# Moving low halves to GpSimd: pooled keys and values, block 0's max-layer values, block 1's tokens

## The chip, the cores and the metric

One core of one Trainium2 chip runs the program. The metric is the time of one execution in microseconds (us) on the device; the span of the profile, from the first to the last instruction, lies inside it. The engines are PE (TensorE, matmuls), PEld (TensorE's weight loads, which overlap PE), DVE (VectorE), ACT (ScalarE), POOL (GpSimd) and SP (SyncE, which issues most transfers).

## What is computed

Three layers follow one another: attention over keys and values that are pooled by 8, a layer that takes the maximum of three products, and a layer with a squared ReLU. The inputs q, k and v are normal draws (q and k of size 0.8, v of 0.1); all is float32.

```python
# q, k, v: (8, 8, 576, 64); pool = 8
k_p = k.reshape(B, H, Sp, pool, D).mean(axis=3)
v_p = v.reshape(B, H, Sp, pool, D).mean(axis=3)
scores = scale * np.matmul(q, k_p.transpose(0, 1, 3, 2))
attn = softmax(scores)                      # over the 72 pooled keys
x = np.matmul(attn, v_p)                    # then (B * S, H * D) = (4608, 512)
h = np.maximum(np.maximum(x @ w1, x @ w2), x @ w3)      # d_ff 768
y = h @ w_out                                           # (4608, 512)
g = np.maximum(y @ w_in, 0.0)                           # d_ff 2048
out = (g * g) @ w_out2
```

## The kernel before

**Halves.** PE multiplies in a rounded float32 form, so each operand is kept as two tiles, a high half (the rounded value) and a low half (the value less its high half), and each product is three matmuls: high by high, high by low, low by high (`PARTS`, line 41). The helper `split_to` (line 120) writes the high half with a copy on ACT (line 121) and the low half with a subtraction on an engine that the caller names (line 122); `split` (line 124) does so for one tile, by default on DVE. `split_scaled` (line 194) does the same for pooled keys and values and multiplies on the way: the scale lies in ACT's copy (line 195) and in DVE's subtraction (line 196).

**First stage.** The 4608 tokens go through attention and the max layer in 12 blocks of 384 (`T1`). `attention(j)` puts the attention steps of block j into a list, each with a due time (line 272): load, prepare, scores with softmax, transposes, values. `moe1(j)` (line 453) is a generator with 22 steps for a block: 18 products (6 slices f of 128 columns by 3 weights, 12 matmuls each, line 465) whose maximum is gathered in `hm` by ACT (line 471) and DVE (line 473), the split of `hm` into `h` after the third (line 475), and 4 products with the output weights (18 matmuls each, line 484). `run` (line 494) emits the steps of all blocks in the order of due times, attention of block j + 1 among the steps of block j. Loads lead by 10 steps, preparation by 4 (line 49). What each engine then does first is set by the planner of the framework, which orders each engine's queue by its own estimate of when an instruction can start; on the chip every queue runs in that order.

**Keys and values.** For each of 32 pairs of heads (4 in each of 8 batches) `prepare_k` (line 219) sums 8 neighbouring keys on DVE into `ks` (line 221; 2 buffers) and writes high and low halves into `kbd`, 64 partitions at a time. `prepare_v` (line 226) does so with values into `vs` (line 228; 2 buffers) and `vst`, for batches 1 to 7, that is 28 pairs; batch 0's values are pooled by matmuls (`pool_v`, line 244). `kbd` and `vst` have one place for each of four pairs, so a new pair waits until the matmuls of the batch before have read it.

**Tokens.** `values` (line 376) multiplies the weights of the softmax by `vst`; from batch 1 on DVE adds two results into `xf` (line 399) and splits it into `x` on line 400. Blocks 0 and 1 (`LIGHT`, `light`) have their queries split on POOL already (line 330); block 1 holds 192 tokens of batch 1, so 4 tiles go through line 400 there.

**Weights.** Weights arrive as 64-bit numbers in 512 KB pieces, in a ring of four `raw` buffers that keys and values share for as long as the weights of the max layer arrive (`place`, line 113). `convert` (line 136) turns a piece into float32 with two ACT copies (lines 148, 149) and two DVE operations (lines 150, 153); POOL writes its low half (line 122). 24 pieces for the max layer come at the start; 32 pieces for the last layer are prepared during blocks 2 to 10, each paced by a one-element POOL copy that reads the newest `hm` (lines 132, 147).

**POOL's queue** before the change: the low halves of queries of blocks 0 and 1, those of all weights, the softmax's multiplication by 1/sum (line 355), and the pacing copies. The second stage, from about 785 us on, uses no POOL.

Of the kernel before, what the change touches and what calls it, by code (L numbers as in the profile page):

```python
# [84 lines left out]
def attention_moe_kernel(ctx: ExitStack, tc: tile.TileContext, q, k, v, vn, w1, w2, w3, wo1, wi2, wo2, out):  # L85
    nc = tc.nc
# [37 lines left out]
    def split(hl, src, engine=nc.vector):  # L124

        split_to(hl[:, 0], hl[:, 1], src, engine)
# [58 lines left out]
    kbd = kv_p.tile([P, NPAIR, 2, 2, SP], F32R, name="kbd")  # L185
# [33 lines left out]
    def prepare_k(p, kr):  # L219
        ks = sm_p.tile([P, SP], F32, tag="ks", name="ks", bufs=2)  # L220
        nc.vector.tensor_reduce(out=ks, in_=kr.rearrange("p (a b) -> p a b", b=POOL), axis=AX.X, op=ALU.add)
        for h in range(2):
            r = slice(h * D, (h + 1) * D)
            split_scaled(kbd[r, p, 0, h], kbd[r, p, 1, h], ks[r], K_SCALE)

    def prepare_v(p, vr):
        vs = sm_p.tile([SP, 2, D], F32, tag="vs", name="vs", bufs=2)
        nc.vector.tensor_reduce(out=vs, in_=vr, axis=AX.X, op=ALU.add)
        split_scaled(vst[:, p, 0:4:3], vst[:, p, 1:3], vs, V_SCALE)

    def load_natural(b):

# [74 lines left out]
    def attend(j, b, s0, n, p, t):  # L307
# [67 lines left out]
        def values():  # L375
# [16 lines left out]
            for h in range(2):  # L392
# [4 lines left out]
                r, o = slice(h * D, (h + 1) * D), slice((1 - h) * D, (2 - h) * D)  # L397
                nc.scalar.activation(xf[r], av[o], AF.Copy)
                nc.vector.tensor_tensor(out=xf[r], in0=av[r], in1=xf[r], op=ALU.add)
            split(x, xf)  # L400

        return load, prepare, softmax, transpose, values

# [49 lines left out]
    def moe1(j):  # L453
# [3 lines left out]
        for f in range(KF1):  # L457
            hm = t_p.tile([P, T1], F32, tag="hm", name="hm")
            h = h_p.tile([P, 2, T1], F32R, tag="h", name="h")
            for e in range(NE):  # L460
                ps = mm_ps.tile([P, T1], F32, tag="ps", name="ps")
                n = 0
                for kk in range(KD):
                    for a, c in PARTS:
                        nc.tensor.matmul(  # L465
                            ps, lhsT=w1_t[f, e][:, a, kk * P : (kk + 1) * P], rhs=x[kk][:, c],
                            start=(n == 0), stop=(n == 3 * KD - 1),
                        )
                        n += 1
                if e == 0:  # L470
                    nc.scalar.activation(hm, ps, AF.Copy)
                else:
                    nc.vector.tensor_tensor(out=hm, in0=ps, in1=hm, op=ALU.max)  # L473
                if e == NE - 1:
                    split(h, hm)
                yield
            hs.append(h)
            now[0] = hm
# [250 lines left out]
```

## Time and profile before

| | us |
|---|---|
| median of 3 runs (1546.5 to 1547.54) | 1547.14 |
| the profiled execution | 1546.39 |
| its span | 1544.7 |
| PE busy in the span (9290 matmuls) | 1509.4 |
| DVE busy | 948.2 |
| ACT busy | 623.5 |
| POOL busy | 199.4 |

An engine's busy time is the sum of its instructions' durations, and an instruction that waits for a port after it has begun counts as busy. Ends of matmuls are modelled. In a line of groups stand the line, engine, operation, what is written and read, the shape and the count, then the sum of busy time, the mean of one in ns, and the idle time of the engine just before them with what ended it. A timeline row begins with the start and the duration in us; in brackets stands the idle time before it and what ended it. "Issue" is time in which an engine waited for nothing that the profile shows.

### The profile page before, as it was taken

To read this page: it belongs to the slowest core of one execution; us is meant where nothing else is said; L and a number is where in the kernel's file an instruction comes from. 1 tells how busy PE (TensorE), PEld (TensorE's weight loads), DVE (VectorE), ACT (ScalarE), POOL (GpSimd) and SP (SyncE) were. 2 spreads that over 40 slices of the span, in tenths; PEclk is the share of its full clock that TensorE was granted. 3 is DMA by queue.
4 is the path that set the end of the run, shared out by engine and by line. 5 is a ranking of instruction groups with operands and counts; after the bars stand their busy time and mean duration, and the time that the engine had idled before them with its cause. 6 is when DMAs were issued, how large, how long until landed. Compare 5 with 4: busy or idle time off the path is not lost.

```text
span 1544.7 us, 25098 instructions
## 1 busy us (share of the span) xinstructions
PE 1509.4 (98%) x9290; PEld 1413.8 (92%) x9290; DVE 948.2 (61%) x1991; ACT 623.5 (40%) x1772; POOL 199.4 (13%) x303
## 2 busy tenths in 40 slices
PE   6899999999999999999999999999999999999998
PEld 4789999999999999999999898988989888999987
DVE  6895678776776767755427555455655546464544
ACT  7875566656666556654212212121212112121211
POOL 5541122222222121322000000000000000000000
PEclk7799999999999999999999999999999999999999
DMA  7552234434334332323475424333333433343331
GB/s 226 159 172 68 76 105 149 145 95 143 122 119 143 97 132 99 102 77 123 135 289 208 150 109 164 110 121 123 112 137 124 150 123 108 111 150 109 137 109 69
DMA packets 80858, 200.87 MB, mean 130 GB/s; under 512 B 9024, under 2 KB 32576, under 8 KB 80736
## 3 DMA queue, kind: packets, MB, share of 16 engines
q1 hardware_dynamic: 73824, 189.83, 36.1%
q10 hardware_dynamic: 6912, 9.44, 1.7%
q8 instruction: 74, 1.21, 0.3%
q14 instruction: 48, 0.39, 0.1%
HBM read 157.29 MB, written 41.94 MB: 129 GB/s over the span
## 4 chain that ended last, share of the span: by engine, by line
PE 85%; DVE 5%; DMA 5%; ACT 2%; issue 2%; SPq 0%; POOL 0%; DVEq 0%; ACTq 0%; POOLq 0%
PE ps L465 25%; PE acc L645 25%; PE ps L600 21%; PE ps L484 9%; PE sc L344 2%; DMA out_dram<-o 2%; PE tr L370 2%; DMA wraw<-in_w_dram 1%; PE av L396 1%; PE av L395 1%; DVE wbits L153 1%; DMA vr<-in_v_dram 1%; DMA wraw<-in_wo_dram 1%; DMA kq<-in_k_dram 1%; DVE wbits L150 0%
## 5 line engine op out<-in xcount | busy, mean ns | idle before, releaser
L465 PE MATMUL ps<-x,w 128*128 128x384 f32 x2592 | 507.6, 343 | 1.8 <-DVE x L122 1.0
L465 PEld LDWEIGHTS ps<-x,w 128*128 128x128 f32 x2592 | 451.1, 191 | 3.9 <-DVE x L122 2.0
L645 PE MATMUL acc<-wo2s,g 128*128 128x512 f32 x1728 | 412.5, 391 | 0.0
L600 PEld LDWEIGHTS ps<-y,wi2s 128*128 128x128 f32 x3024 | 370.4, 188 | 12.5 <-PE ps L600 3.4
L600 PE MATMUL ps<-y,wi2s 128*128 128x256 f32 x3024 | 376.8, 280 | 2.8 <-DVE s L629 2.2
L645 PEld LDWEIGHTS acc<-wo2s,g 128*128 128x128 f32 x1728 | 316.2, 188 | 62.6
L121 ACT ACTIVATE g<-c 128x512 fp32r<-128x512 f32 x144 | 90.8, 630 | 410.4 <-DVE c L611 403.6
L617 DVE TENSOR_TENSOR s<-ps,s 128x512 f32<-128x512 f32 x72 | 49.8, 692 | 262.2 <-PE ps L600 261.6
L484 PE MATMUL ps<-h,wo 128*128 128x384 f32 x864 | 165.2, 339 | 0.5 <-DVE hm L473 0.4
L484 PEld LDWEIGHTS ps<-h,wo 128*128 128x128 f32 x864 | 148.9, 188 | 1.3 <-DVE hm L473 0.7
L617 DVE TENSOR_TENSOR c<-ps,s 128x512 f32<-128x512 f32 x144 | 99.0, 688 | 24.9 <-PE ps L600 21.7
L355 POOL TENSOR_TENSOR ss<-ss,st 128x144 f32<-128x144 f32 (+3 forms) x144 | 74.2, 517 | 308.7 <-DVE st L354 238.6
L473 DVE TENSOR_TENSOR hm<-ps,hm 128x384 f32<-128x384 f32 x144 | 79.5, 552 | 54.2 <-PE ps L465 50.3
L349 ACT ACTIVATE ss<-sc,st 128x72 f32<-128x72 f32 (+1 forms) x320 | 98.3, 314 | 33.3 <-DVE st L346 30.8
L122 DVE TENSOR_TENSOR g<-c,g 128x512 fp32r<-128x512 f32 x144 | 98.8, 686 | 17.3 <-ACT g L121 16.4
L611 DVE SCALAR_TENSOR_TENSOR c<-c 128x512 f32<-128x512 f32 x144 | 99.0, 688 | 2.2
L373 DVE TENSOR_TENSOR pt<-tr,pt 72x256 fp32r<-72x256 f32 (+1 forms) x160 | 61.5, 387 | 52.6 <-ACT pt L372 51.2
L344 PEld LDWEIGHTS sc<-kbd,qs 128*128 128x128 f32 (+1 forms) x480 | 73.3, 191 | 12.3 <-issue 5.3
L344 PE MATMUL sc<-kbd,qs 128*128 128x144 f32 (+1 forms) x480 | 73.9, 269 | 9.2 <-ACT kbd L195 5.3
L372 ACT ACTIVATE pt<-tr 72x256 fp32r<-72x256 f32 (+1 forms) x160 | 56.4, 355 | 58.9 <-PE tr L370 57.4
L370 PE MATMUL tr<-ident,ss 128*72 128x128 f32 (+1 forms) x320 | 59.2, 271 | 13.9 <-DVE pt L373 8.8
L349 ACT ACTIVATION_READ_ACCUMULATOR ss<-sc,st 128x1 f32 (+1 forms) x320 | 63.4, 198 | 0.0
(78 smaller groups left out, 1247.0 us busy)
## 6 DMA issues: line engine op xcount, KB each, us to landing
wo2s<-wo_dram SPq DMA_DIRECT2D x144, 512.0 KB
wi2s<-wi_dram SPq DMA_DIRECT2D x24, 512.0 KB
wraw<-in_wo_dram SPq DMA_DIRECT2D x22, 512.0 KB
wraw<-in_w_dram SPq DMA_DIRECT2D x18, 512.0 KB
y_dram<-ys ACTq DMA_DIRECT2D x48, 192.0 KB
out_dram<-o SPq DMA_DIRECT2D x36, 256.0 KB
wraw<-in_wi_dram SPq DMA_DIRECT2D x16, 512.0 KB
wi_dram<-wraw SPq DMA_DIRECT2D x16, 512.0 KB
```

Source lines behind the costliest of these rows:

```text
L121: nc.scalar.activation(hi, src, AF.Copy)
L122: engine.tensor_tensor(out=lo, in0=src, in1=as_f32(hi), op=ALU.subtract)
L344: nc.tensor.matmul(src[:, i], lhsT=lhsT, rhs=kbd[:, p, l], start=(n == 0), stop=(n == 2))
L349: nc.scalar.activation(ss[:, i, h], src[:, i, h], AF.Exp, bias=st[:, 0, i, h : h + 1], accum_out=st[:, 1, i, h : h + 1],)
L370: nc.tensor.transpose(tr[:, h, :m], sms[c][:, h], ident[:m, :m])
L465: nc.tensor.matmul(ps, lhsT=w1_t[f, e][:, a, kk * P : (kk + 1) * P], rhs=x[kk][:, c], start=(n == 0), stop=(n == 3 * KD - 1),)
L473: nc.vector.tensor_tensor(out=hm, in0=ps, in1=hm, op=ALU.max)
L484: nc.tensor.matmul(ps, lhsT=wo1_t[kk][:, a, d * P : (d + 1) * P], rhs=hs[kk][:, c], start=(n == 0), stop=(n == 3 * KF1 - 1),)
L600: nc.tensor.matmul(bank[:, u * HT : (u + 1) * HT], lhsT=wi2_t[2 * gr + u][i][:, a, o + kk * P : o + (kk + 1) * P], rhs=y_t[j][m][:, c, kk] ...
L611: nc.vector.scalar_tensor_tensor(out=c, in0=c, scalar=0.0, in1=c, op0=ALU.max, op1=ALU.mult)
L617: nc.vector.tensor_tensor(out=c, in0=bank, in1=other, op=ALU.add)
L645: nc.tensor.matmul(acc_t[j][2 * half + i], lhsT=g[:, a, u * HT + i * P : u * HT + (i + 1) * P], rhs=wo2_t[j, 4 * gr + 2 * u + h][:, c], st ...
```

## The change

`prepare_k` and `prepare_v` multiply `ks` and `vs` by their scale in place on POOL, and then split them with `split_to`, whose low half is written by POOL; ACT's copies lose their scale. `split_scaled` remains for batch 0's values (`pool_v`). The low half of `x` is written by POOL in blocks 0 and 1 where a batch is 1 or later (4 tiles), and that of `h` in block 0 (6 tiles).

```diff
     def prepare_k(p, kr):
         ks = sm_p.tile([P, SP], F32, tag="ks", name="ks", bufs=2)
         nc.vector.tensor_reduce(out=ks, in_=kr.rearrange("p (a b) -> p a b", b=POOL), axis=AX.X, op=ALU.add)
+        nc.gpsimd.tensor_scalar_mul(ks, ks, K_SCALE)
         for h in range(2):
             r = slice(h * D, (h + 1) * D)
-            split_scaled(kbd[r, p, 0, h], kbd[r, p, 1, h], ks[r], K_SCALE)
+            split_to(kbd[r, p, 0, h], kbd[r, p, 1, h], ks[r], nc.gpsimd)
 
     def prepare_v(p, vr):
         vs = sm_p.tile([SP, 2, D], F32, tag="vs", name="vs", bufs=2)
         nc.vector.tensor_reduce(out=vs, in_=vr, axis=AX.X, op=ALU.add)
-        split_scaled(vst[:, p, 0:4:3], vst[:, p, 1:3], vs, V_SCALE)
+        nc.gpsimd.tensor_scalar_mul(vs, vs, V_SCALE)
+        split_to(vst[:, p, 0:4:3], vst[:, p, 1:3], vs, nc.gpsimd)
...
-            split(x, xf)
+            split(x, xf, nc.gpsimd if light else nc.vector)
...
                 if e == NE - 1:
-                    split(h, hm)
+                    split(h, hm, nc.vector if j else nc.gpsimd)
```

## Rows read from the trace of the kernel before

**Rows 1.** Windows: PE, PEld, DVE, ACT, POOL busy (count), clock, DMA share, GB/s.
```profile
0.00:118.00 118.00, 93.41 (x468) 79.49 (x469) 97.87 (x197) 90.10 (x297) 62.23 (x62) 0.84 0.58 184
118.00:735.00 617.00, 613.25 (x3787) 604.33 (x3786) 421.01 (x1120) 366.82 (x1199) 137.14 (x241) 1.00 0.34 112
```

**Rows 2.** Windows of stretches within the first 118 us, the same columns.
```profile
100.00:105.00 5.00, 2.97 (x15) 2.37 (x16) 4.94 (x7) 3.08 (x7) 3.35 (x3) 0.88 0.34 82
105.00:110.00 5.00, 5.00 (x27) 5.00 (x26) 5.00 (x13) 4.34 (x17) 0.32 (x1) 0.78 0.57 168
80.00:100.00 20.00, 18.93 (x115) 17.49 (x112) 19.40 (x40) 18.29 (x50) 11.31 (x10) 1.00 0.57 194
```

**Rows 3.** Chain of work, 0 to 118 us: start, us, what.
```profile
13.58 0.10 DVE kbd L196
13.72 0.94 DVE kbd L196
...
69.31 4.82 DMA wraw<-in_w_dram
...
98.97 2.01 DVE h L122
...
113.46 0.47 DVE h L122
```

**Rows 4.** Timeline of PE: two waits in the first block.
```profile
101.90 0.36 PE L395 MATMUL av<-pt,vst 72*128 72x192 f32 x1 [2.09 <-DVE xf L399]
...
115.11 4.11 PE L484 MATMUL ps<-h,wo 128*128 128x384 f32 x22 [0.36 <-DVE hm L473]
```

**Rows 5.** Groups of DVE, 0 to 118 us, shapes apart.
```profile
L150 DVE SCALAR_TENSOR_TENSOR wbits<-wbits,wraw 128x512 int32<-128x512 int32 x24 | 21.7, 913 | 1.2 <-ACT wraw L149 0.9 <-issue 0.2
L153 DVE SCALAR_TENSOR_TENSOR wbits<-wraw,wbits 128x512 int32<-128x512 int32 x24 | 18.7, 784 | 0.1
...
L196 DVE SCALAR_TENSOR_TENSOR kbd<-ks,kbd 64x72 fp32r<-64x72 f32 x18 | 7.0, 389 | 0.7 <-ACT kbd L195 0.4
...
L122 DVE TENSOR_TENSOR h<-hm,h 128x384 fp32r<-128x384 f32 x5 | 4.2, 844 | 0.4 <-ACT h L121 0.4
...
L196 DVE SCALAR_TENSOR_TENSOR vst<-vs,vst 72x128 fp32r<-72x128 f32 x4 | 1.6, 396 | 0.0
```

**Rows 6.** Groups of POOL, 0 to 118 us, shapes apart.
```profile
L122 POOL TENSOR_TENSOR qs<-qr,qs 128x192 fp32r<-128x192 f32 x8 | 6.9, 862 | 2.7 <-issue 1.5 <-ACT qs L121 1.1
...
L122 POOL TENSOR_TENSOR qs<-kq,qs 128x384 fp32r<-128x384 f32 x4 | 4.8, 1192 | 10.6 <-ACT qs L121 10.6
```

**Rows 7.** Groups of the whole span, shapes apart.
```profile
L122 DVE TENSOR_TENSOR g<-c,g 128x512 fp32r<-128x512 f32 x144 | 98.8, 686 | 17.3 <-ACT g L121 16.4
...
L355 POOL TENSOR_TENSOR ss<-ss,st 128x144 f32<-128x144 f32 x84 | 39.7, 475 | 200.2 <-DVE st L354 161.8 <-ACT pt L372 8.2 <-ACT ss L349 6.9
...
L132 POOL COPY wraw<-hm 1x1 f32<-1x1 f32 x32 | 7.8, 244 | 20.8 <-DVE hm L473 16.1 <-DMA wi_dram<-wraw 2.5 <-DMA wo_dram<-wraw 1.2
```

**Rows 8.** Timeline of DVE and POOL, 64 to 68 us.
```profile
64.04 3.57 DVE L150 SCALAR_TENSOR_TENSOR wbits<-wbits,wraw 128x512 int32<-128x512 int32 x2
64.28 0.98 POOL L355 TENSOR_TENSOR ss<-ss,st 96x288 f32<-96x288 f32 x1 [2.06 <-DVE st L354]
65.22 0.59 POOL L122 TENSOR_TENSOR qs<-qr,qs 128x192 fp32r<-128x192 f32 x1
65.77 1.29 POOL L122 TENSOR_TENSOR w<-wbits,w 128x512 fp32r<-128x512 f32 x1
```

**Rows 9.** Timeline of PE, 460 to 640 us: its longest wait after 118 us.
```profile
498.29 1.16 PE L344 MATMUL sc<-kbd,qs 128*128 128x144 f32 x6 [1.89 <-ACT ss L349]
```

**Rows 10.** Timeline of DVE, 222.5 to 225 us.
```profile
223.21 0.48 DVE L196 SCALAR_TENSOR_TENSOR kbd<-ks,kbd 64x72 fp32r<-64x72 f32 x2
...
223.73 0.75 DVE L221 TENSOR_REDUCE ks<-kr 128x72 f32<-128x576 f32 x1
```

**Rows 11.** Waits, 118 to 735 us: engine, line, for what, us, times, longest.
```profile
POOL wraw L132 <- DVE hm L473: 16.1, 7, 9.8
```

## The prediction

> **What bounds the kernel now.** I read the windows by stage first. From 118 to 735 us PE is busy for 613.25 of 617 us at clock 1.00 (2.4 GHz), while DVE is busy for 421 and POOL for 137 [rows 1]: PE is the bound there, and what another engine gives back is lost in its own slack. The second stage holds nothing for this change: the two windows' 62.23 and 137.14 us are all of POOL's 199.4 us [rows 1]. What is left is the first 118 us. There PE is busy for only 93.41 us at a mean clock of 0.84, and DVE, ACT and POOL for 97.87, 90.10 and 62.23 us [rows 1]. The chain of waits for this stretch shows what sets the order: weights' transfers (the piece at 69.31 takes 4.82 us), ACT's and DVE's conversions of them, and pieces of DVE in every part of it [rows 3]. From 80 to 100 us DVE is busy for 19.40 of 20 us [rows 2], and the two PE waits that can be read behind it are both for DVE: 2.09 us at 101.90 and 0.36 us at 115.11 [rows 4].
>
> Third, the groups and the timeline show that DVE's time there is partly waiting for POOL. The DVE operation of line 150 with two inputs in SBUF takes a mean of 913 ns in this stretch [rows 5], where the same size of two-input operation takes 686 ns in the second stage, in which POOL is idle [rows 7]. At 64.04 two of them take 3.57 us, while three POOL instructions run one after another from 64.28 to 67.06 [rows 8]: the second stood until POOL was through. So POOL's work is not beside DVE's; part of it stands in DVE's way.
>
> **What is removed.** In the first 118 us DVE loses 18 key halves of 389 ns (7.0), 4 value halves of 396 (1.6) and 5 low halves of h of 844 (4.2) [rows 5]: 12.8 us; the sixth h half and the four halves of x come at the edge of this stretch or behind it. Later it loses 46 key halves of 240 ns (the pair at 223.21 takes 0.48 [rows 10]) and 24 value halves, each between that and 396 ns, 11 us and 6 to 10; PE bounds that part, so they are worth nothing directly.
>
> **What is added.** POOL's prices bound the new ones from both sides. A key half (64x72) and the multiplications (72 or 128 columns, one tensor input) lie between a one-element copy, 244 ns, and the softmax product on 128x144, 475 ns [rows 7]; I take 0.36 for the first and 0.30 for the second, about the middle, for both are smaller than the upper row and have its kind of reads. A value half (72x128) lies between 475 and the 862 ns of 128x192 [rows 6]; I take 0.47, since its width is nearer to 144. A half of h is the 128x384 row itself, 1192 ns, and a half of x the 128x192 row, 862 [rows 6]. In the first 118 us that is 18 x 0.36 + 13 x 0.30 + 4 x 0.47 + 5 x 1.19 = 18.3 us (15 with the lower rows, 24 with the upper), so POOL goes from 62 to about 80 us of 118. After 118 us it is 46 x 0.36 + 47 x 0.30 + 24 x 0.47 and about 4.6 for the last h and the x halves, 47 us on POOL's 137 of 617: a third of its time, no bound.
>
> **What this does to DVE.** Lines 150 and 153 stand 24 x (913 - 686) + 24 x (784 - 686) ns = 7.8 us above their undisturbed time [rows 5, 7] for 62 us of POOL [rows 1], 0.13 us for each. By that share 18 us more of POOL delays what is left on DVE by 2.3 us; with none in the way it is 0, with every added microsecond in front of a waiting DVE operation it is 18, at the upper prices 24. I take 3, near the measured share, a little above it as POOL gets fuller. DVE then comes out 12.8 - 3 = about 10 us lighter (between 13 lighter and 11 heavier).
>
> The Trainium skill, page "SBUF — State Buffer", section "Who interferes with whom", speaks against the change at this point: a DVE instruction with two SBUF inputs and a GpSimd instruction that reads SBUF hold one pair of ports as an exclusive lock, and the later one blocks fully. The trace agrees: the 3.57 us at 64.04 [rows 8]. By that rule at its worst DVE would get 5 us heavier; by the share in the rows it gets 10 us lighter.
>
> **What of it reaches the end.** Not 10 us. In the chain nine pieces are instructions that leave DVE, from 13.58 to 113.46; they sum to 4.9 us, 2.01 and 0.94 the largest [rows 3]. Against them stand, on the path: the multiplications of the first pairs of keys, ahead of ACT's copy (two on the path, 0.6 us); POOL's longer h halves, ahead of the output products (1.19 against 0.84, 0.35 us); the delay of DVE, 3 us, of which perhaps half falls on the chain (1.5). Left is 2.5 us. What is late next is the weight ring: transfers of about 5 us each whose buffers come free behind ACT and DVE [rows 3], and ACT, busy for 18.29 of 20 us from 80 to 100 [rows 2], whose work stays. And PE, from 80 us on, is 95% busy [rows 2], so it can take back little but the wait before 101.90 and the slow clock behind it. I take 1.5 us of the 2.5.
>
> **The added waits.** ACT's copies of ks and vs now stand behind a POOL multiplication, and the low halves behind POOL's queue. In it stand pacing copies that wait for DVE's `hm`, up to 9.8 us [rows 11], and softmax products. The emission leads by four steps (line 49), some 11 us with 617 us for ten blocks of 22 steps, so I cost this wait at nothing; without that lead it would be the 9.8 us. The second wait is less plain: `ks` and `vs` have two buffers, and the sum for the next pair but one may only overwrite when the low half has read. In the trace the sum on DVE begins at 223.73, right behind the half at 223.21 on the same engine [rows 10]. Now the sum waits for POOL, and behind it on DVE's queue stand `hm`'s maximum (line 473), which frees PE's banks, and the softmax's maximum (line 346). DVE is busy for 421 of 617 us [rows 1], so I cost it at 0, with up to 5 us for the range. In the other direction DVE's relief after 118 us can at most remove the 3.75 us that PE is not busy there [rows 1].
>
> **The sum.** Span 1544.7 - 1.5 + 0 = 1543.2. The profiled execution took 1546.39, so 1.7 us lie outside the span; the median is 0.75 above it: 1543.2 + 1.7 + 0.7 = 1545.6 us. A measurement of this kernel tells about 0.2% from no change, 3.1 us; so the forecast is a small gain that counts as no change.
>
> **The rivals.**
> *DVE's relief arrives whole.* The 4.9 us of the chain go, PE no longer waits at 101.90, and the clock does not fall behind that wait: 100 to 110 us ran at 0.88 and 0.78, a loss of 5 x 0.12 + 5 x 0.22 = 1.7 us [rows 2]. Together 6.6 us: 1540.5. For it speaks that PE waits for DVE at the two places shown; against it that POOL is slower for the same work and the ring's transfers stay.
> *The shared port becomes the bound (slower).* The place is 80 to 100 us, where DVE is at 19.40 and POOL at 11.31 of 20 us [rows 2]. About three halves of h, two of values and one pair of keys fall there: DVE loses 3 x 0.84 + 2 x 0.40 + 2 x 0.39 = 4.1 us, POOL gets 3 x 1.19 + 2 x 0.47 + 2 x 0.36 + 3 x 0.30 = 6.1. If all of it stands before a waiting DVE operation, DVE falls back by 2.0 us instead of gaining, and PE waits a second time as at 101.90, 2.09 us [rows 4] with 1.7 of slow clock: 5.8 us, 1552.9. It decides from the point where more than two thirds (4.1 of 6.1) of POOL's added time blocks DVE; the measured share is 0.13.
> *The sum waits for POOL (slower).* After 118 us DVE stands in front of a sum of keys or values until POOL has written a low half, and PE's banks stay full. One such stop costs what PE's longest wait there cost, 1.89 us [rows 9], and about as much again in clock by the 1.7 above; 56 sums have this wait (30 of 32 of keys, 26 of 28 of values), and one or two stops that show give 4 to 7 us: 1551. It decides from the point where POOL's queue is behind DVE's by more than PE's banks hold.
> *The change does not do what it says:* the planner orders all queues anew, so the gain could vanish and the order alone decide: 1547.
>
> **How the numbers follow.** The forecast has 0.40 (its own range 1543.5 to 1548), whole relief 0.25, the port 0.13, the wait for POOL 0.14, no effect 0.08. Of the forecast a sixth reaches past 0.2% faster. Faster by over 0.2%: 0.25 + 0.07 = 0.32; slower: 0.13 + 0.14 = 0.27; within: 0.33 + 0.08 = 0.41. The range leaves about one in ten out on each side: 1539.5 to 1552.
>
> **What would show it.** Right: DVE's busy time in the first stage lower by about 25 us, POOL's higher by 55 to 70; kbd halves on POOL near 0.36 us; lines 150 and 153 slightly above 913 and 784 ns; the first product of block 0's output weights a microsecond or two earlier, and the same length from there on. The port rival shows in line 150 well over 1 us and a wait of PE before 118 us longer than 2.09; the wait rival in DVE's lines 221 and 228 waiting for POOL's line 122 by more than a few microseconds in total, and PE below 613 us of 617 in the middle stretch. The prediction is wrong if the middle stretch moves by more than 4 us, or if POOL's small instructions cost above 0.5 us.

## The result and the profile after

The changed kernel takes 1563.09 us (median of 5, 1560.53 to 1565.95) against 1546.68 for the kernel before in the same rounds (1546.13 to 1547.54): a ratio of 1.0103, 95% interval 1.0089 to 1.0118. It is 1.0% slower, above the range that was forecast. The profiled execution has a span of 1561.4 us, 16.7 us more than before. In the changed kernel, lines from the middle of the file on stand two lower (L344 is now L346, L465 is L467, L484 is L486).

I first marked the ends of the program's parts in both traces: the end of the last half of the first token block x (`x3`), the end of the last output product of blocks 0 and 11, and the end. In us:

```
                                  before   before, 2nd profile   after
x3                                 61.72         61.79           72.60
end of block 0                    126.85        125.45          138.82
from there to the end of block 11 657.88        656.06          659.32
second stage                      759.96        762.25          763.24
```

12.0 of the 16.7 us are lost by the end of block 0, 10.9 of them before the first token block is complete. The middle stretch has 1.4 us, the second stage 3.3; but a second profile of the unchanged kernel has 762.25 us there, so 2.3 us of those 3.3 lie within what one kernel shows from run to run. The question is what happens in the first 73 us.

The windows that answer to [rows 1] and to the 80 to 100 us of [rows 2], same columns; the stretch of 80 to 100 us and the middle stretch are moved by the 12 us, so that they hold about the same work:

```profile
0.00:118.00 118.00, 86.55 (x415) 73.93 (x415) 82.30 (x143) 83.30 (x270) 75.89 (x95) 0.77 0.54 173
80.00:100.00 20.00, 19.21 (x120) 18.08 (x119) 16.32 (x28) 13.87 (x40) 13.35 (x17) 1.00 0.52 160
92.00:112.00 20.00, 17.30 (x98) 16.16 (x97) 18.58 (x29) 17.44 (x45) 12.87 (x13) 0.91 0.48 158
130.00:747.00 617.00, 611.66 (x3772) 603.39 (x3773) 404.80 (x1046) 368.20 (x1203) 194.13 (x359) 0.99 0.34 111
```

DVE is 15.6 us lighter in the first 118 us, but so are PE (by 6.9 us) and ACT (by 6.8): the stage isn't faster, everything in it is late. From 80 to 100 us, where DVE was full before [rows 2], it is now busy for 16.32 us, but those 20 us hold earlier work than before; in the stretch moved by 12 us DVE is busy for 18.58 of 20, hardly less than the 19.40 of before. The mean clock falls from 0.84 to 0.77. Up to the end of block 0 PE's busy time rises by 2.4 us (102.3 to 104.7) and its idle time by 9.5 (24.6 to 34.1), so the lower clock can hold only the smaller part of the loss.

**Where the first 10 us go.** First the kernel before, four rows of its start (the timeline; PE, DVE, ACT):

```profile
6.25 1.99 PE L344 MATMUL sc<-kbd,qs 128*128 128x144 f32 x8 [0.44 <-DVE kbd L196]
8.27 0.61 DVE L346 TENSOR_REDUCE st<-sc 128x6 f32<-128x432 f32 x1 [2.08 <-PE sc L344]
8.36 6.27 PE L250 MATMUL vp<-natural,sums 128*72 128x512 f32 x10
8.91 0.32 ACT L349 ACTIVATE ss<-sc,st 128x72 f32<-128x72 f32 x1 [3.71 <-DVE st L346]
```

Then the same in the kernel after:

```profile
4.52 0.39 POOL L222 TENSOR_SCALAR ks<-ks 128x72 f32<-128x72 f32 x1 [0.47 <-DVE ks L221]
5.64 0.46 PE L346 MATMUL sc<-kbd,qs 128*128 128x144 f32 x1 [5.64 <-ACT kbd L121]
6.21 0.74 POOL L122 TENSOR_TENSOR kbd<-ks,kbd 64x72 fp32r<-64x72 f32 x2
7.75 5.52 PE L252 MATMUL vp<-natural,sums 128*72 128x512 f32 x8 [1.65 <-DMA natural<-in_vn_dram]
12.70 1.41 PE L346 MATMUL sc<-kbd,qs 128*128 128x144 f32 x8
13.87 0.75 DVE L221 TENSOR_REDUCE ks<-kq 128x72 f32<-128x576 f32 x1 [1.04 <-POOL kbd L122]
14.35 0.55 ACT L121 ACTIVATE kbd<-ks 64x72 fp32r<-64x72 f32 x2 [1.71 <-POOL ks L222]
14.54 0.60 DVE L348 TENSOR_REDUCE st<-sc 128x6 f32<-128x432 f32 x1
17.62 0.30 ACT L351 ACTIVATE ss<-sc,st 128x72 f32<-128x72 f32 x1
19.58 1.13 PE L346 MATMUL sc<-kbd,qs 128*128 128x144 f32 x4 [3.30 <-ACT ss L351]
```

The low halves of the first pair are done at 6.95 us, 0.8 us after before's. But in PE's queue pooled values now stand between the first score and the other eight, and on DVE the sums of the next pairs stand ahead of the maximum. The exponentials begin at 17.62 instead of 8.91 us: ACT had nothing else to do at 9 us (it waits 5.7 us for a query there now), and at 17.6 they stand among weights' conversions; PE waits 3.30 us for them. PE's waits for exponentials, 0 to 118 us, before and after (for what: us, times, longest):

```profile
PE sc L344 <- ACT ss L349: 1.5, 3, 0.7
PE sc L346 <- ACT ss L351: 7.0, 3, 3.3
```

**The shared port on the path.** The row like [rows 8] now lies at 32 us:

```profile
32.12 1.28 POOL L122 TENSOR_TENSOR w<-wbits,w 128x512 fp32r<-128x512 f32 x1
32.48 2.90 DVE L150 SCALAR_TENSOR_TENSOR wbits<-wbits,wraw 128x512 int32<-128x512 int32 x1
33.37 0.90 POOL L357 TENSOR_TENSOR ss<-ss,st 128x432 f32<-128x432 f32 x1
34.24 0.59 POOL L122 TENSOR_TENSOR qs<-qr,qs 128x192 fp32r<-128x192 f32 x1
...
36.52 0.61 PE L372 MATMUL tr<-ident,ss 128*72 128x128 f32 x2 [4.94 <-DVE pt L375]
```

One conversion on DVE stands until three POOL instructions are through, and PE waits 4.94 us for the half of `pt` behind it; the conversion's own delay, 2.90 us less the 0.68 of an undisturbed one, is 2.2 us of that. Before, such rows were there too (3.57 us at 64.04 [rows 8]), but PE waited nowhere this long for DVE. At 45.56 it is the other way round: a multiplication of 0.53 us elsewhere takes 3.04 on POOL while DVE runs conversions from 45.39 to 48.21. At the place that the prediction named for this rival, moved by the same 12 us, it shows as well:

```profile
97.56 4.15 DVE L153 SCALAR_TENSOR_TENSOR wbits<-wraw,wbits 128x512 int32<-128x512 int32 x2
98.04 0.91 POOL L122 TENSOR_TENSOR vst<-vs,vst 72x128 fp32r<-72x128 f32 x1
98.91 1.01 POOL L122 TENSOR_TENSOR h<-hm,h 128x384 fp32r<-128x384 f32 x1
99.89 1.27 POOL L122 TENSOR_TENSOR w<-wbits,w 128x512 fp32r<-128x512 f32 x1
```

Two of the three POOL instructions here are new. PE then waits 1.71 us for DVE at 102.03, no longer than the 2.09 of before [rows 4].

**What the new instructions cost.** The groups that answer to [rows 5] and [rows 6]: whole span for POOL, up to the end of block 0 (138.82 us) for DVE. The last row is of the kernel before, up to its end of block 0, and answers to the one above it (the softmax's addition on its sums):

```profile
L122 POOL TENSOR_TENSOR kbd<-ks,kbd 64x72 fp32r<-64x72 f32 x64 | 27.9, 436 | 34.0 <-ACT kbd L121 27.1 <-PE tr L372 4.2
L230 POOL TENSOR_SCALAR vs<-vs 72x128 f32<-72x128 f32 x28 | 21.3, 762 | 28.3 <-DVE vs L229 23.7 <-DVE st L355 2.9 <-DVE st L356 1.6
L222 POOL TENSOR_SCALAR ks<-ks 128x72 f32<-128x72 f32 x32 | 15.4, 481 | 23.1 <-DVE ks L221 10.1 <-DVE st L356 7.6 <-DVE st L355 4.4
L122 POOL TENSOR_TENSOR vst<-vs,vst 72x128 fp32r<-72x128 f32 x28 | 15.2, 542 | 45.7 <-ACT vst L121 45.5
L122 POOL TENSOR_TENSOR h<-hm,h 128x384 fp32r<-128x384 f32 x6 | 7.7, 1281 | 1.1 <-ACT h L121 1.1
...
L153 DVE SCALAR_TENSOR_TENSOR wbits<-wraw,wbits 128x512 int32<-128x512 int32 x24 | 23.5, 988 | 0.2
L150 DVE SCALAR_TENSOR_TENSOR wbits<-wbits,wraw 128x512 int32<-128x512 int32 x24 | 20.2, 850 | 7.5 <-ACT wraw L149 7.5
L355 DVE TENSOR_SCALAR st<-st 96x4 f32<-96x4 f32 x8 | 6.2, 770 | 0.9 <-ACT ss L351 0.9
L353 DVE TENSOR_SCALAR st<-st 96x4 f32<-96x4 f32 x8 | 3.3, 408 | 1.0 <-ACT ss L349 0.8
```

And the waits of DVE for POOL from 130 to 747 us, the middle stretch (engine, line, for what: us, times, longest):

```profile
DVE ks L221 <- POOL kbd L122: 3.7, 7, 1.0
DVE vs L229 <- POOL vst L122: 2.5, 7, 0.5
```

14 sums wait for POOL there, 6.2 us in all, the longest 1.0. PE is busy for 611.66 us of those 617, for 613.25 before. By the letter of the prediction's signs for this rival (more than a few microseconds of waits, PE below 613 us) it shows, at 1.6 us.

### The profile page after: what moved, and what is told of

Read it like the earlier page. It is cut to its first block, busy times and chain, and to the rows that moved or that the text cites. A ratio compares the mean times of both kernels' runs of the same rounds, so it can differ in the third digit from the quotient of the medians.

```text
span 1561.4 us, 25173 instructions
## 1 busy us (share of the span) xinstructions
PE 1512.4 (97%) x9290; PEld 1417.9 (91%) x9290; DVE 927.2 (59%) x1889; ACT 625.3 (40%) x1772; POOL 280.2 (18%) x465
## 4 chain that ended last, share of the span: by engine, by line
PE 53%; DMA 2%; DVE 1%; issue 0%; ACT 0%; SPq 0%; DVEq 0%; ACTq 0%
PE acc L647 24%; PE ps L602 20%; PE ps L467 5%; PE ps L486 2%; DMA out_dram<-o 2%; DVE c L619 0%; DMA wo2s<-wo_dram 0%; DVE s L631 0%; PE tr L372 0%; PE sc L346 0%; ACT o L659 0%; PE av L398 0%; PE av L397 0%; SPq L660 0%; DVE s L619 0%
## 5 line engine op out<-in xcount | busy, mean ns | idle before, releaser
L467 PE MATMUL ps<-x,w 128*128 128x384 f32 x2592 | 509.7, 344 | 2.5 <-ACT x L121 1.1
L467 PEld LDWEIGHTS ps<-x,w 128*128 128x128 f32 x2592 | 452.3, 191 | 3.7 <-ACT x L121 1.8
L602 PEld LDWEIGHTS ps<-y,wi2s 128*128 128x128 f32 x3024 | 370.5, 188 | 15.6 <-PE ps L602 3.9
L486 PE MATMUL ps<-h,wo 128*128 128x384 f32 x864 | 166.3, 339 | 2.3 <-POOL h L122 0.9
L486 PEld LDWEIGHTS ps<-h,wo 128*128 128x128 f32 x864 | 148.7, 188 | 3.1 <-ACT ys L492 1.2
L375 DVE TENSOR_TENSOR pt<-tr,pt 72x256 fp32r<-72x256 f32 (+1 forms) x160 | 61.6, 386 | 59.6 <-ACT pt L374 59.1
L346 PEld LDWEIGHTS sc<-kbd,qs 128*128 128x128 f32 (+1 forms) x480 | 74.1, 191 | 18.6 <-ACT ss L351 10.5
L346 PE MATMUL sc<-kbd,qs 128*128 128x144 f32 (+1 forms) x480 | 76.2, 270 | 14.6 <-ACT ss L351 9.0
L121 ACT ACTIVATE h<-hm 128x384 fp32r<-128x384 f32 x72 | 37.6, 523 | 69.4 <-DVE hm L475 69.1
```

Of the source, the lines that this page charges most:

```text
L121: nc.scalar.activation(hi, src, AF.Copy)
L346: nc.tensor.matmul(src[:, i], lhsT=lhsT, rhs=kbd[:, p, l], start=(n == 0), stop=(n == 2))
L467: nc.tensor.matmul(ps, lhsT=w1_t[f, e][:, a, kk * P : (kk + 1) * P], rhs=x[kk][:, c], start=(n == 0), stop=(n == 3 * KD - 1),)
L486: nc.tensor.matmul(ps, lhsT=wo1_t[kk][:, a, d * P : (d + 1) * P], rhs=hs[kk][:, c], start=(n == 0), stop=(n == 3 * KF1 - 1),)
L602: nc.tensor.matmul(bank[:, u * HT : (u + 1) * HT], lhsT=wi2_t[2 * gr + u][i][:, a, o + kk * P : o + (kk + 1) * P], rhs=y_t[j][m][:, c, kk] ...
```

## The experiments

A time is the median; the ratio is to the kernel before in the same rounds, whose medians lay between 1546.1 and 1547.9 us. "Block 0" is the end of block 0 in the profile against the 126.85 us of before. A single profile moves by 1 to 3 us (the second profile of before: -1.4 at block 0), so the verdicts rest on ratios.

| kernel | median | ratio, 95% interval | block 0 |
|---|---|---|---|
| changed kernel | 1563.09 | 1.0103 (1.0089 to 1.0118) | +12.0 |
| keys and values alone | 1559.31 | 1.0080 (1.0065 to 1.0095) | +7.1 |
| h and x alone | 1552.76 | 1.0037 (1.0023 to 1.0050) | +2.5 |
| keys alone | 1555.34 | 1.0063 (1.0043 to 1.0083) | +4.0 |
| change without batch 0's keys | 1555.43 | 1.0059 (1.0042 to 1.0075) | +4.8 |
| first pair of keys alone | 1557.71 | 1.0074 (1.0059 to 1.0089) | +7.4 |
| change without the first pair | 1563.73 | 1.0114 (1.0099 to 1.0129) | +16.3 |
| h alone | 1552.46 | 1.0039 (1.0025 to 1.0054) | +3.5 |
| h as zeros from POOL | 1547.88 | 1.0004 (0.9994 to 1.0014) | -2.7 |
| first scores held back, no work moved | 1551.77 | 1.0034 (1.0022 to 1.0045) | +8.4 |
| keys and values from batch 2 on | 1549.16 | 1.0021 (1.0011 to 1.0030) | +0.2 |
| change, multiplications on DVE | 1553.38 | 1.0050 (1.0035 to 1.0065) | +2.7 |
| before, POOL reads h once more | 1552.29 | 1.0029 (1.0018 to 1.0041) | +2.6 |
| zeros for h, in POOL's turn | 1550.30 | 1.0020 (1.0009 to 1.0031) | -0.7 |
| change, batch 0's multiplications on DVE | 1556.72 | 1.0061 (1.0045 to 1.0076) | +7.9 |
| change without batch 0's keys and h | 1556.55 | 1.0056 (1.0039 to 1.0073) | +5.5 |
| before, block 1's queries to DVE | 1550.99 | 1.0021 (1.0011 to 1.0031) | +4.8 |
| before, blocks 0 and 1's queries to DVE | 1553.80 | 1.0039 (1.0024 to 1.0054) | +5.5 |

**Parts of the change.** The first four take the change apart.

*Keys and values alone:* x and h stay with DVE.

```diff
-            split(x, xf, nc.gpsimd if light else nc.vector)
+            split(x, xf)
-                    split(h, hm, nc.vector if j else nc.gpsimd)
+                    split(h, hm)
```

> Keys and values alone go to GpSimd; x and h stay on VectorE. Theory A (the first pair's low halves come late on GpSimd, the planner puts the pooling matmuls ahead of its scores, and the softmax of pair 0 is pushed from ScalarE's idle time into its full stretch; GpSimd's lock on the shared port adds the rest): nearly the whole loss stays, 1558 to 1563 us, pair 3's tokens (x3) at about 72 us as in the changed kernel. Theory B (the halves of h fill GpSimd and the port between 75 and 118 us, the rival of the prediction): half of the loss or more goes, 1553 or less.

*h and x alone:* values as before, and keys likewise:

```diff
-        nc.gpsimd.tensor_scalar_mul(vs, vs, V_SCALE)
-        split_to(vst[:, p, 0:4:3], vst[:, p, 1:3], vs, nc.gpsimd)
+        split_scaled(vst[:, p, 0:4:3], vst[:, p, 1:3], vs, V_SCALE)
```

> The halves of h in block 0 and of x in block 1 alone go to GpSimd. Theory A: the loss lies ahead of these instructions (x3 is 10.9 us late before the first of them), so 1545 to 1549. Theory B: 1553 or more.

*Keys alone:* x, h and values as before (the two edits above), keys as in the change.

> Keys alone go to GpSimd, values stay on VectorE. Theory A: the order at the start is that of the changed kernel, so at least half of the loss: 1554 to 1562. Theory C (the values' multiplication, which took 3.04 us at its worst in the first 50 us, and its low halves are the load that locks VectorE out): 1547 to 1551, the loss is in the values.

*The change without batch 0's keys:*

```diff
-        nc.gpsimd.tensor_scalar_mul(ks, ks, K_SCALE)
+        if b:
+            nc.gpsimd.tensor_scalar_mul(ks, ks, K_SCALE)
...
+                split_scaled(kbd[r, p, 0, h], kbd[r, p, 1, h], ks[r], K_SCALE)
```

> The whole change, but the four key pairs of batch 0 keep the way of before (scaled by ScalarE and VectorE). Theory A: the start has its old order again, x0 is late by at most 1 us and x3 by at most 4, 1547 to 1552. If instead the load on the shared port makes the loss, whatever the order: x3 is 8 us late or more and the time 1556 or more.

Each part costs by itself: 0.80, 0.37, 0.63%; the halves add to 1.17, a little over the whole's 1.03. Taking back batch 0's four pairs of keys, 12 of the 162 instructions that POOL gets, returns 0.44% of the 1.03. For h and x alone, and for the change without batch 0's keys, the time lies between what the two theories said. In the second x3 is only 1.6 us late, as the theory of the order had it, and block 0 4.8: most of that loss comes behind x3.

**The start: work or order?**

*The first pair alone* on POOL, three instructions:

```diff
+        new = b == 0 and p == 0
+        if new:
+            nc.gpsimd.tensor_scalar_mul(ks, ks, K_SCALE)
...
+            if new:
+                split_to(kbd[r, p, 0, h], kbd[r, p, 1, h], ks[r], nc.gpsimd)
```

> The kernel before, with one thing of the change: of batch 0's first pair of heads (of 64 key halves the first two) the multiplication and the two low halves are on POOL; 3 instructions of some 0.4 us each. In this kernel PE's queue begins as that of the changed kernel does (one score, four matmuls that pool values, then the other eight scores of the first pair), in the kernel before with nine scores. Theory A (the loss at the start comes from the changed order of the queues: the first pair's scores and exponentials slide from ACT's idle time behind the pooled values): token block x0 ends 2 to 4 us later and the whole is 3 to 8 us slower, 1550 to 1555. Theory B (the load on POOL and the port lock delay DVE): three instructions of 1.2 us in all can't cost more than that, 1546 to 1548.

*The change without the first pair:*

```diff
+        new = b or p
```

> The whole change, but the first pair of heads of batch 0 keeps its multiplication and low halves on DVE as before. PE's queue then begins with nine scores as in the kernel before. Theory A (order at the start): it takes back about what leaving all four pairs of batch 0 on DVE took back, 1554 to 1557 against 1563 for the whole change. Theory B (load on POOL): only 3 of 12 instructions of that batch are taken back, so at most 2 us, 1561 to 1563.

*The first scores held back:*

```diff
+        if early_v:
+            nc.vector.tensor_copy(kbd[:, p, 1, 0, :2], early_v.pop()[:, 0, :2])
         for h in range(2):
...
+        if b == 0:
+            early_v.append(tiles[0])
```

Its copy also leaves two columns of values in the rows that belong to the other head of the first pair, which stay zero otherwise. Four matmuls of pooled values then stand ahead of the first pair's eight scores, as in the kernel with the first pair alone; in the changed kernel it is eight.

> The kernel before with all work on its old engine; a single two-column copy on DVE ahead of the first pair's second key half reads the first piece of natural values, which lands at about 7.7 us, so the first pair's scores slide behind pooled values as in the changed kernel. POOL gets nothing. Theory A (the late start of the first pair's scores and exponentials is the cost at the start, whoever causes it): x0 ends 2 to 5 us later and the whole is 5 to 11 us slower, 1552 to 1558, near the 1557.7 of the kernel with the first pair alone on POOL. Theory B (POOL's added instructions cost it): 1546 to 1549.

Three moved instructions cost 10.7 us and block 0 7.4: it isn't their work. With no instruction moved, and the first pair's scores late by a wait, block 0 ends 8.4 us late. Rows of the held-back kernel (line 350 are scores, 355 the exponentials):

```profile
8.31 3.66 PE L256 MATMUL vp<-natural,sums 128*72 128x512 f32 x4 [2.70 <-DMA natural<-in_vn_dram]
10.98 2.24 PE L350 MATMUL sc<-kbd,qs 128*128 128x144 f32 x8
15.95 0.32 ACT L355 ACTIVATE ss<-sc,st 128x72 f32<-128x72 f32 x1
```

The exponentials begin 7.0 us later than before (8.7 in the changed kernel). So in these two kernels a late first pair costs about 8 us up to block 0's end, though it was made late in different ways. It is no fixed price: with all multiplications on DVE (below) the exponentials are 5.2 us late and block 0 ends 2.7 us late. That the held-back kernel ends only 5.6 us slower has another place: it loses nothing in block 7, which takes 59.6 us there and 65.0 in the kernel before, in which PE waits for an exponential [rows 9] and the clock falls behind it (a mean of 0.76 from 498 to 505 us). The second profile of before has 63.8 us there. Why this order of queues misses that stop is open.

The change without the first pair contradicts the simple form of this: its scores come first again (the eight at 6.03 us), and it gains nothing. Its rows show what else the three other pairs meet:

```profile
16.46 0.75 DVE L221 TENSOR_REDUCE ks<-kq 128x72 f32<-128x576 f32 x1 [2.92 <-POOL kbd L122]
19.58 1.98 PE L351 MATMUL sc<-kbd,qs 128*128 128x144 f32 x8 [1.98 <-POOL kbd L122]
21.06 0.55 ACT L121 ACTIVATE kbd<-ks 64x72 fp32r<-64x72 f32 x2 [1.88 <-POOL ks L224]
```

The sum on DVE waits for POOL's half, PE's scores wait for POOL's half, ACT's copy waits for POOL's multiplication, and POOL works through queries' halves and a softmax product between them. So the runs fit two ways to lose the start: the order, and POOL's turn in a chain that went DVE, ACT, DVE before and now goes DVE, POOL, ACT, POOL. The second is read from these rows; no run gives the keys POOL's turn and keeps the old order.

**The multiplications.**

*The change with all multiplications on DVE:*

```diff
-        nc.gpsimd.tensor_scalar_mul(ks, ks, K_SCALE)
+        nc.vector.tensor_scalar_mul(ks, ks, K_SCALE)
...
-        nc.gpsimd.tensor_scalar_mul(vs, vs, V_SCALE)
+        nc.vector.tensor_scalar_mul(vs, vs, V_SCALE)
```

> The whole change, but the two multiplications of the sums by their scale are on DVE, in front of ACT's copies; the low halves stay on POOL. Theory P (POOL's queue, in which the multiplications of the first pairs stand behind queries' halves, delays ACT's copies and so the tokens): x3 ends 3 to 6 us earlier than in the changed kernel, 1557 to 1560. Theory A (order of the first pair's scores, which stays as in the changed kernel): 1561 to 1564.

*With batch 0's four alone on DVE:*

```diff
+        (nc.gpsimd if b else nc.vector).tensor_scalar_mul(ks, ks, K_SCALE)
```

> The whole change, but the four multiplications of batch 0's keys (of 60 multiplications) are on DVE; all low halves stay on POOL. With all multiplications on DVE the time was 1553.4. If the multiplications at the start are what counts (ACT's copies of the first four pairs wait for POOL), these four bring most of those 10 us: 1553 to 1557. If the later ones count: 1559 to 1563.

All 60 on DVE bring back half of the loss, 0.53% of 1.03, more than either theory had; four of them bring 0.42%, as the theory of the start had it, and no less than taking all of batch 0's keys back (0.44). PE's waits for exponentials up to 118 us show what they buy: 7.0 us in the changed kernel, 6.6, 7.2 and 9.4 in the other three in which the first pair's multiplication is on POOL (keys and values, keys, first pair alone), 3.3 with the first scores held back, 1.4 with four multiplications on DVE, 0.3 with all, 1.5 before. In the kernel with all on DVE the multiplication of the first pair takes 0.20 us and the first exponentials start at 14.08, 3.5 us earlier than in the changed kernel, though PE's queue begins with one score there too; but only four pooled matmuls follow it there, not eight, so this edit changed the order as well. The Trainium skill, page "GPSIMD Engine Reference", section "Engine selection", has one-input elementwise work on GpSimd at roughly line rate; here the same 128x72 multiplication took 0.39 us on POOL undisturbed and 0.20 on DVE, which doesn't bear that out for so small a tile.

**h.**

*h alone* on POOL, in the kernel before:

```diff
-                    split(h, hm)
+                    split(h, hm, nc.vector if j else nc.gpsimd)
```

> The kernel before, with only the low halves of h in block 0 (6 tiles of 128x384) on POOL. Theory L (these halves lock DVE's weight conversions out of the shared port between 75 and 118 us, and stand behind POOL's queue): block 0 ends 2 to 3 us later, the whole is 3 to 6 us slower, 1550 to 1553, about as h and x together (1552.8). Theory R (DVE's relief of 6 x 0.84 us counts): 1543 to 1546.

*h as zeros:*

```diff
+                    if j:
+                        split(h, hm)
+                    else:
+                        nc.scalar.activation(h[:, 0], hm, AF.Copy)
+                        nc.gpsimd.memset(as_f32(h[:, 1]), 0.0)
```

> As the kernel with h alone on POOL, but in block 0 the low half of h is left out: POOL writes zeros into that tile instead of the difference, an instruction that reads nothing, so that PE still waits for an instruction of POOL's queue. The result of block 0 lacks that half's part. Theory L (the lock counts: POOL's reading instruction in front of DVE's conversions): the loss goes, 1545 to 1548. Theory Q (POOL's queue counts: the half stands behind weights' halves and products that POOL does first, and PE waits): most of the loss stays, 1549 to 1552.

*POOL reads h once more:*

```diff
                     split(h, hm)
+                    if j == 0:
+                        nc.gpsimd.tensor_tensor(out=hm, in0=hm, in1=as_f32(h[:, 0]), op=ALU.subtract)
```

> The kernel before, h's low half on DVE as ever; in block 0 POOL then does the same 128x384 subtraction once more in place over the spent maximum, for nobody. So POOL reads as much as in the kernel with h on POOL, but DVE isn't relieved and PE doesn't wait for POOL. Theory L (the shared port: POOL's reading instructions delay DVE's conversions): 3 to 6 us slower than before, 1549 to 1552. Theory Q (PE and others wait for POOL's turn): 1546 to 1548.

*Zeros in POOL's turn*, in front of that memset:

```diff
+                        nc.gpsimd.tensor_copy(h[:1, 1, :2], as_f32(h[:1, 0, :2]))
```

> As the kernel in which POOL writes zeros for block 0's low half of h (that part of h is left out again), but with a two-element POOL copy of the high half in front, so that POOL's instruction stands in its queue where the real one would, waits for the same maximum and ACT's copy, and takes only some 0.7 us of which hardly any is reading. Theory Q (waiting for POOL's turn): most of the 5 us, 1550 to 1552. Theory L (reading through the shared port): 1546 to 1548.

Of the 0.39% that h costs on POOL, 0.29 come with the reading alone, for nobody and with DVE's halves kept; with the turn alone it is 0.20, the lower end of what that theory said; with neither 0.04 (the plain memset waits for no maximum and runs ahead, so it tests both at once). Both act, and their intervals overlap. Rows of h alone show the reading, in both directions:

```profile
99.33 1.15 POOL L355 TENSOR_TENSOR ss<-ss,st 96x288 f32<-96x288 f32 x1 [2.29 <-DVE st L354]
99.99 3.27 DVE L153 SCALAR_TENSOR_TENSOR wbits<-wraw,wbits 128x512 int32<-128x512 int32 x1
100.45 1.30 POOL L122 TENSOR_TENSOR wo<-wbits,wo 128x512 fp32r<-128x512 f32 x1
101.71 1.00 POOL L122 TENSOR_TENSOR h<-hm,h 128x384 fp32r<-128x384 f32 x1
...
111.37 3.61 POOL L122 TENSOR_TENSOR h<-hm,h 128x384 fp32r<-128x384 f32 x1 [2.78 <-ACT h L121]
```

And the kernel in which POOL reads h for nobody shows who pays, weights' halves and PE behind them:

```profile
108.30 4.33 POOL L122 TENSOR_TENSOR wo<-wbits,wo 128x512 fp32r<-128x512 f32 x1 [2.60 <-ACT wo L121]
...
113.55 2.02 POOL L122 TENSOR_TENSOR wo<-wbits,wo 128x512 fp32r<-128x512 f32 x1
...
115.62 0.44 PE L486 MATMUL ps<-h,wo 128*128 128x384 f32 x1 [1.41 <-POOL wo L122]
```

The Trainium skill, page "SBUF — State Buffer", section "Who interferes with whom", says that the one that issues first keeps the shared pair for its whole instruction and that "Issue order, not op shape, decides who blocks"; these rows agree (3.27 us for DVE at 99.99, behind three POOL instructions; 3.61 for POOL at 111.37, while DVE ran operations with two inputs at 111.84 and 113.57 and a sum between them), and show besides that the wait lasts over several instructions of the other side.

**The rest.**

*Keys and values from batch 2 on;* the queues up to block 0 are those of before:

```diff
+        new = b > 1
```

> The change for keys and values of batches 2 to 7 alone (48 key halves, 24 value halves and their multiplications on POOL); batches 0 and 1, x and h as before. The queues up to about 118 us are those of the kernel before. Prediction (the middle stretch is bound by PE, so it neither gains nor loses): 1546 to 1549, PE's length from block 0 to block 11 within 1.5 us. The rival (the sum on DVE waits for POOL's low half and PE's banks stay full): 4 to 7 us, 1551 to 1554.

*The change without batch 0's keys and without h*, two of the edits above:

```diff
+        if b:
...
+                    split(h, hm)
```

> The whole change without its two parts that were seen to cost: batch 0's keys and block 0's h stay on DVE; keys of batches 1 to 7, all values and x are on POOL. If the two parts are the loss (8 and 5 us) this is 1547 to 1551, near the 1549.2 of batches 2 to 7 alone; if batch 1's keys and values, which fall into the first stage too, cost as much by themselves: 1552 to 1555.

*The kernel before, profiled again*, with no edit.

> The kernel before, profiled a second time. In the first profile the second stage lasts 759.9 us from the end of block 11 to the end of the span. If the 2 to 4 us that all variants show there beyond it (mostly at the eighth output block) are the spread of single executions, this profile has some of them too; if the variants cause them, it has 760 again.

In the steady part the move costs 0.1 to 0.3%, little but clear of nothing, and just above the 1546 to 1549 us that were expected: the sums' waits there are as short as in the changed kernel (ks 3.5 us, longest 0.6). The sum of the two suspects doesn't hold: with batch 0's keys and h both back on DVE the loss is 0.56%, the same as with the keys alone back (0.59). The difference to the move from batch 2 on, 0.35%, is that of batch 1's keys and values and of x, which run in the first stage too. There line 153 waits more (0 to 130 us; 1086 ns for 784 in [rows 5]) and line 150 less (757 for 913), together 921 for 848. PE's waits for DVE's half of `pt` up to 118 us show where that lands: 16.3 us in this kernel and 15.9 in the change without batch 0's keys, 7.2 before, 10.4 in the changed kernel. By these rows the two lose their time behind DVE's delayed queue and not behind late exponentials; which of the moved instructions delay it, no run here separates.

The second profile of before puts the second stage down to spread, as far as 2.3 of the 3.3 us go.

**The opposite move.** If POOL's reads and DVE's two-input operations are one resource, work that goes from POOL to DVE should gain.

```diff
-            split(qs[0], qr[0], nc.gpsimd if light else nc.vector)
+            split(qs[0], qr[0], nc.vector if j else nc.gpsimd)
```

> The kernel before with the opposite move: the low halves of block 1's queries (8 tiles of 128x192) go from POOL, where they take 862 ns each, to DVE, where that shape takes about 350. The first nine scores stay where they are. Theory S (POOL's reads and DVE's two-input operations are one resource; a piece costs more of it on POOL): 6.9 us of POOL against 2.8 of DVE, block 0 ends 0 to 4 us earlier, 1543 to 1547. Theory D (DVE's load is the bound, as the prediction had it): block 0 ends 2 to 3 us later, 1548 to 1550.

*And block 0's too:*

```diff
+            split(qs[0], qr[0])
```

> As the run before, and block 0's four query halves (128x384, 1192 ns on POOL, about 540 on DVE) go to DVE too. PE's queue now begins with one score and pooled values, as in the changed kernel, though POOL has less to do. Theory S with order (the late first pair costs, whoever causes it): 1549 to 1556. If only POOL's load counts: 1540 to 1546.

It doesn't gain; both are slower. In the second, POOL is busy for 56.95 us of the first 118 (62.23 in [rows 1]) and line 150 waits less than before, 743 ns for 913 (0 to 125 us). Still block 0 ends 5.5 us late: its first exponentials start at 14.47. In the first, with the start of before, line 153 rises to 952 ns and line 150 falls to 781, 866 for 848 together, though POOL has 6.9 us less to do. So the wait at the port isn't a share of POOL's time; it depends on what happens to stand side by side.

The theory that DVE's load bounds the start comes closer, though its 1550 us was passed by 1.0. Up to the end of block 0 DVE is busy for 103.2 us before, for 107.7 and 108.2 in these two, 4.5 and 5.0 more, and block 0 ends 4.8 and 5.5 us later. DVE's idle time up to there is nearly the same in all these: 23.7 us before, 23.6 in its second profile, 24.0 and 24.2 here, 24.0 with h as zeros (DVE 3.0 us lighter, block 0 2.7 us earlier), 23.6 where POOL reads h once more. It is 27.0 and 29.1 with h on POOL, 29.0 with the first scores held back, and 43.0 in the changed kernel. So the profiles fit a start that DVE bounds in the kernel before, and that the change turned into one bound by waits; it is a reading of profiles and not a test. No version tried beats the kernel before.

## Why the prediction was wrong

- **What bounds the kernel: it fits the kernel before, not the one after.** The middle stretch holds little, as said: 1.4 us in the profile, 0.21% (3 us) when done alone. The first 118 us hold most of the loss. I read DVE's 19.40 of 20 us as the bound there, and DVE's nearly constant idle time fits that. But DVE got lighter by 7.4 us up to the end of block 0 (103.2 to 95.8 us), and the stage got 12 us longer: after the change it is bound by a chain through all engines with little lead, and no engine's load.
- **What is removed: right.** The halves that were named run on POOL, and DVE is 7.4 us lighter up to the end of block 0; why not 10, is in the delay.
- **What is added: too low.** A key half took 436 ns (0.36), the multiplications 481 and 762 (0.30), a value half 542 (0.47), a half of h 1281 (1192); only x was cheaper, 716 (862). Undisturbed it is 0.39 for a key multiplication, 0.37 for a key half, 0.53 for a value multiplication: the key half was priced right, the multiplications too low (that of values lies above the upper bound of 0.475), and the rest is waiting after they had begun. Up to the end of block 0 the moved pieces are 24 us by the prices of the prediction and take 33.6; POOL's busy time rises by only 25 (63.8 to 88.8), for its older instructions got shorter. By the prediction's own test, a small POOL instruction above 0.5 us, it is wrong here.
- **DVE's delay: too low.** The 48 operations of lines 150 and 153 rose from a mean of 848 ns to 919, 3.4 us; 3 was said for all of DVE. The softmax's additions, which have one input, weren't counted and were held as well: 17 take 9.3 us up to the end of block 0, 19 took 6.8 before, where an undisturbed one takes 0.15. That is about 3 us more, in the direction of the 7.4 us that came for 10. And the delay is no share of POOL's time (919 with 88.8 us of POOL, 1078 with 87.4 in the change without batch 0's keys, where that is 11 us): that the forecast of the conversions came out is luck.
- **What of it reaches the end: the step that failed.** I set the gain of nine pieces of the chain, 4.9 us, against 0.6 us of multiplications and 0.35 of h. The multiplications weigh most: taking four of them back returned 0.42%, some 6.5 us, and all 60 8.2 us (0.53%), each with about 0.2% of uncertainty. With them went PE's waits for exponentials, from 7.0 us to 1.4 and 0.3. The 0.35 us of h were 0.39% (5.4 us) when h alone was moved. A row's duration isn't the price of a new link in a chain; its price is the place that it takes in another engine's queue, and what slides behind it.
- **The added waits: nearly right later, wrong at the start.** That the emission leads by four steps, so that ACT's wait for POOL costs nothing, nearly holds from batch 2 on (0.21%). Batch 0 has no lead: its keys, scores and exponentials are made as soon as their transfers land, and there the waits that I listed (ACT's copies behind the multiplication 1.71 us, the sum behind POOL's half 1.04) are on the path. The 9.8 us that I gave for a case without lead come near the loss by luck: they are a wait of the pacing copies, the first of which runs at 184.9 us.
- **The rivals.** The whole relief didn't come. The shared port did, with PE waiting 4.94 us at 32 us, a place that wasn't named; at the place that was named two conversions took 4.15 us, and PE's wait behind them, 1.71, was no longer than before. The sum that waits for POOL came at 16 us in one variant (2.92), and after 118 us at 6.2 us in all, for which PE lost 1.6. The order was named as a rival that takes the gain away; that it can cost 8 us up to block 0 by itself (the first scores held back) was not thought of.
- **What stays open.** How the 12 us divide between order, turn and port in the changed kernel itself; PE's waits for exponentials (5.5 us more than before) and for `pt` (3.2 more) are the largest that can be named. The parts don't add up (keys and h back on DVE is no better than keys alone back), and each edit gives all queues a new order, so a run of one part is never that part alone. Keeping the old order with the new work wasn't tried.

## What to carry over

Before work is moved to an idle engine, look at the first use of what it makes: where the pipeline has no lead yet, a new engine in the chain costs its place in that engine's queue, not its duration. With a planner that orders queues by its estimates, read the first twenty instructions of each queue after the edit; here three moved instructions put pooled values ahead of the first scores, and ACT's idle time around 9 us couldn't be had again. Taking work from the engine that bounds a stage helps only if it doesn't come back as waits in that engine's own queue: DVE was 7.4 us lighter here and stood idle for 19 us more.

## What the runs showed of the hardware

- A DVE operation with two inputs in SBUF and a POOL instruction that reads SBUF hold each other up for several instructions on end, in both directions: 3.27 us for an operation of 0.68 on DVE (h alone), 4.33 for one of 1.30 on POOL (the kernel in which POOL reads h once more).
- An operation on DVE with one input was held too: the softmax's addition on 96x4, 0.15 us undisturbed, took 2.48 us at 82.28 in the changed kernel, while POOL instructions of 1.30 and 1.01 us ran from 82.45 on.
- POOL's memset of 128x384, which reads nothing, took a mean of 418 and of 420 ns in two kernels (6 times each), in the same stretch in which the subtraction of that size took from 1.00 to 3.61 us.
- One kernel's second stage, with no POOL instruction in it, took 759.96 us in one execution and 762.25 in another.
